# Turning a batch's last 64 logits with small products, between two heads' values

## The chip, the cores and the metric

One core of a Trainium2 chip runs the whole program. The metric is the device time of one execution in microseconds; below it is the median of three runs. A profile of one execution shows what every engine did.

## The reference

Decaying causal attention over 8 batches of 8 heads (576 tokens, head width 64), whose output (4608 x 512) goes through a soft mixture of 8 experts with 4 slots each:

```
scores = scale * (q @ k^T) + cum[i] - cum[j], masked above the diagonal
attn   = softmax(scores);  x = attn @ v             (all heads side by side: 512 columns)
logits = x @ phi                                     (4608 x 32)
d = softmax of logits over all tokens   ->  slot_input = d^T @ x
slot_out = relu(slot_input @ w1) @ w2                (per expert)
c = softmax of logits over the 32 slots ->  out = c @ slot_out
```

So every batch's logits are needed twice: against the running maximum over tokens (to dispatch tokens to slots), and token by token over the 32 slots (to combine slots).

## The kernel before, in words

The order of every engine's work is written out by hand: an engine issues its instructions in the order in which the program's lines name it, and waits on semaphores for the others.

**The main loop** (lines 725 to 865) goes over g = 1 to 31, two heads ("pair") at a time, four pairs to a batch. In a pair, TensorE computes the first scores of heads to come (`s1`, line 230, into three score banks `s` that rotate), the second scores of the pair's own heads (`s2`, lines 283 and 284, into a ring of three banks), turns the output of the pair before (`px`, line 342) and ends with the value products (`s3`, line 315), head 0's and then head 1's. ScalarE takes the exponentials (`expo`, line 290), rounds keys and queries of a later pair (`round_k`, `round_q`, lines 183 and 188) and copies; VectorE takes row maxima (`tops`) and normalizes heads (`norm`, lines 330 to 335); GpSimd masks (`causal`) and subtracts low parts (`low_k`, `low_q`).

**The logits of a batch b** lie as 32 slots on each of four lane groups; 576 tokens are 4 x 128 and a last 64, which stands in columns 128 to 192 of lanes 0 to 31. The steps are spread over the next batch's pairs, numbered w = 0 to 3: at the end of w = 0 the product with phi (`logits`, line 389); in w = 1 the copy to `LG` (`weigh`), the maximum (`mgroup`, `mtop`) and its broadcast to all lanes by four products 32 wide and 2 columns long (`mcast`, lines 420 to 424), the weights `EX = exp(LG - max)` (`weigh2`, line 431), the running sum `lrun` (`total`, line 446), and `tokens`; in w = 2 `dispatch` (line 475), which uses the turned weights `LD`.

**`tokens`** turns both tables from slots on lanes to tokens on lanes, in a score bank called `tk`: three 128-column turns by the identity (lines 456, 457, 459), the second of EX's columns 128 to 256 alone. That one turn serves both tables, since the last 64 weights and the last 64 raw logits had been copied to other lanes of `EX` columns 192 to 256 before (GpSimd copies, lines 397 and 432). The turned rows of the first table go to `LD` (line 464, ScalarE), those of the second are read from the bank by `combine(b, 0)` on VectorE (lines 495, 496), which stands early in w = 2 and frees the bank. `combine` steps 1 and 2 follow with the next batch.

**The last batch** does the same in the tail (lines 870 to 905), where LD is copied on VectorE, where `split` and `cols` turn the combinations of all batches into weights of the output products (lines 696, 711), and where `tokens(b, 0)` stands between the expert products (line 938).

A float32 product is issued as two passes, each with its own weight load; a turn is issued once.

Of the kernel before, what the change touches and what calls it, by code (L numbers as in the profile page):

```python
# [9 lines left out]
AF = mybir.ActivationFunctionType  # L10
# [65 lines left out]
def attn_softmoe(ctx: ExitStack, tc: tile.TileContext, qk, v, f, phi, w1, w2, cst, out):  # L76
    nc = tc.nc
# [102 lines left out]
    def round_k(g, *hs):  # L180
        if pair(g):
            for h in hs or range(2):
                nc.scalar.copy(WA[g % 3][0:64, S * h : S * h + S], RAW[g % 3][64:128, h])  # L183

    def round_q(g, *hs):
        if pair(g):
            for h in hs or range(2):
                nc.scalar.copy(YA[g % 3][0:64, h, 64:640], RAW[g % 3][0:64, h])  # L188
# [202 lines left out]
    def weigh(b):  # L391
        if batch(b):
            plg = st["lg", b]
            if b < B - 1:
                nc.scalar.copy(LG[:, 0:128], plg[:, 0:128])
                nc.scalar.copy(LG[0:32, 128:192], plg[0:32, 128:192])
                nc.gpsimd.tensor_copy(EX[96:128, 192:256], LG[0:32, 128:192])  # L397
            else:
                nc.scalar.copy(LG[:, 0:192], plg[:, 0:192])
                nc.gpsimd.tensor_copy(EX[96:128, 192:256], LG[0:32, 128:192])  # L400

    def mgroup(b):
        if not batch(b):
# [22 lines left out]
    def weigh2(b):  # L426
        if not batch(b):
            return
        mb = st["mb", b]
        if b < B - 1:  # L430
            nc.scalar.activation(EX[:, 0:192], LG[:, 0:192], AF.Exp, bias=mb[:, 1:2], accum_out=mb[:, 2:3])
            nc.gpsimd.tensor_copy(EX[0:32, 192:256], EX[0:32, 128:192])
        else:
            nc.scalar.activation(EX[:, 0:192], st["lg", b][:, 0:192], AF.Exp, bias=mb[:, 1:2])
            nc.vector.tensor_copy(EX[0:32, 192:256], EX[0:32, 128:192])
        if b > 0:
            nc.scalar.activation(mb[:, 3:4], st["mb", b - 1][:, 1:2], AF.Exp, bias=mb[:, 1:2], scale=-1.0)

    def total(b):
        if not batch(b):  # L440
            return
        mb = st["mb", b]
        if b == 0:
            nc.scalar.copy(lrun, mb[:, 2:3])
        elif b < B - 1:
            nc.scalar.activation(lrun, lrun, AF.Identity, scale=mb[:, 3:4], bias=mb[:, 2:3])
        else:
            nc.vector.scalar_tensor_tensor(lrun, in0=lrun, scalar=mb[:, 3:4], in1=mb[:, 2:3], op0=ALU.mult, op1=ALU.add)

    def tokens(b, *ns):  # L450

        if not batch(b):
            return
        pm = turn() if b == B - 1 else scratch(False, f"tk{b}")
        if 1 in ns:
            nc.tensor.transpose(pm[:, 0:128], EX[:, 0:128], ident)
        nc.tensor.transpose(pm[:, 128:256], EX[:, 128:256], ident)
        if 0 in ns:
            nc.tensor.transpose(pm[:, 256:384], LG[:, 0:128], ident)
        if 0 in ns:  # L460
            st["tok", b] = pm
        if 1 in ns:
            copy = nc.scalar.copy if b < B - 1 else nc.vector.tensor_copy
            copy(LD, pm[:, 0:160].rearrange("p (t s) -> p t s", t=NBLK))
# [74 lines left out]
    nc.gpsimd.memset(WA[0][96:98].bitcast(F32), -1.0)  # L539
    nc.gpsimd.memset(YA[0][0:64, :, 0:64].bitcast(F32), 0.0)  # L540
    nc.gpsimd.memset(LG[:, 128:256], -1.0e30)
    nc.gpsimd.memset(EX[:, 192:256], 0.0)
    nc.vector.tensor_scalar(fx, fx, 1e-4, 1.0, op0=ALU.max, op1=ALU.min)
    nc.scalar.activation(fx, fx, AF.Ln)
    for h in range(2):
# [137 lines left out]
    def split(b, *parts):  # L683

        if 0 in parts:
            if b < 2:
                CW[b] = tp.tile([P, NBLK, 2, 2, NS], F32R, name=f"cw{b}")
            else:
                spare = quarter[NRES - 9 + b][:, 0 : 4 * NBLK * NS].bitcast(F32R)
                CW[b] = spare.rearrange("p (t o r s) -> p t o r s", t=NBLK, o=2, r=2)  # L690
        hi, lo = (CW[b][:, :, :, r] for r in range(2))
        two = ctok[:, b].rearrange("p t (o s) -> p t o s", o=1).broadcast_to([P, NBLK, 2, NS])
        if 0 in parts:
            nc.scalar.copy(hi, two)
        if 1 in parts:
            nc.vector.tensor_tensor(lo, two, hi.bitcast(F32), op=ALU.subtract)
# [28 lines left out]
    for g in range(1, NG):  # L725
        h0, h1 = 2 * g, 2 * g + 1
        u0, u1 = h0 + 3, h0 + 4
        b, w = divmod(g - 4, NPAIR)
        c = b - 1 if w == 0 else b if (b, w) == (B - 2, 3) else None
        if g < 4:  # L730
            load_v(g + 1)
            load_qk(g + 3)
        else:
            load_qk(g + 3)
            load_v(g + 1)
        if w == 1:
            weigh(b)
        low_q(h0 + 2)
        low_q(h1 + 2)
        s2(h0, 0)  # L740
        expo(h0, 0)
        norm(h0 - 1)
        if w == 1:
            mgroup(b)
        if w == 2:
            combine(b, 0)
        s1(u0, 2)
        tops(u0, 2)
        s2(h0, 1)
        expo(h0, 1)  # L750
        s1(u0, 3)
        tops(u0, 3)
        s2(h0, 2)
        expo(h0, 2)
        if g > 1:
            px(g - 1, 0)
            px(g - 1, 3)
        else:
            round_k(3, 0)
            round_q(3, 0)  # L760
        s1(u0, 0, 1)
        tops(u0, 0, 1)
        if g > 1:
            px(g - 1, 1)
        s2(h0, 3)
        if g > 1:
            xcopy(g - 1, (0, 3))
            px(g - 1, 2)
            xcopy(g - 1, (1, 2))
        s2(h0, 4)  # L770
        s1(u0, 4, 5)
        s2(h0, 5)
        expo(h0, 3)
        tops(u0, 4, 5)
        causal(h0)
        low_k(h0 + 2)
        if w == 1:
            mtop(b)
        s2(h1, 0)
        expo(h1, 0)  # L780
        if g == 1:
            for t in (0, 3, 1, 2):
                px(0, t)
        px(g - 1, 4)
        if g == 1:
            xcopy(0, (0, 3))
            xcopy(0, (1, 2))
        if g == 1:
            xcopy(0, (4,))
        s1(u1, 2)  # L790
        tops(u1, 2)
        s2(h1, 1)
        expo(h1, 1)
        s1(u1, 3)
        tops(u1, 3)
        s2(h1, 2)
        mturn(g + 1)
        mrows(g + 1)
        expo(h1, 2)
        if g > 1:  # L800
            xcopy(g - 1, (4,))
        s1(u1, 0, 1)
        tops(u1, 0, 1)
        s2(h1, 3, 4)
        s1(u1, 4, 5)
        s2(h1, 5)
        expo(h1, 3)
        tops(u1, 4, 5)
        causal(h1)
        low_k(h1 + 2)  # L810
        if g == 1:
            round_k(3, 1)
            round_q(3, 1)
        load_cum(g + 3)
        dup_q(g + 2)
        dup_k(g + 2)
        if 2 <= g < NRES + 2:
            wload(g - 2)
        if g == 29:
            sides[2].close()  # L820
            p2 = fresh(ctx, "p2", 2)
            wstream(*p2, RAW[30 % 3])
        if g == 30:
            sides[1].close()
            xp = ctx.enter_context(tc.tile_pool(name="xp", bufs=1))
            X.append(xp.tile([P, NBLK, 256], F32, name="X3"))
            p0 = fresh(ctx, "p0", 1)
            p1 = fresh(late, "p1", 3)
            wstream(*p0, *p1, RAW[31 % 3])
        if g == 31:  # L830
            sides[0].close()
            with tc.using_default_side("right"):
                tp = ctx.enter_context(tc.tile_pool(name="tp", bufs=1))
            cT = tp.tile([P, sum(CUT)], F32R, name="cT")
            wstream(tp.tile([P, QW], F32, name="w36"))
        if w == 1:
            mcast(b)
        if c is not None:
            combine(c, 1)
        if w == 2 and b < B - 2:  # L840
            dispatch(b, *range(NBLK))
        if g == NG - 1:
            st["lg", B - 1] = scratch(False, f"lg{B - 1}")
            nc.vector.memset(st["lg", B - 1][:, 128:192], -1.0e30)
        round_k(g + 3)
        if w == 1:
            weigh2(b)
            total(b)
        round_q(g + 3)
        if c is not None:  # L850
            combine(c, 2)
        s3(g, VALUES[:30])
        norm(h0)
        if g == 31:
            logits(B - 1, 0, 1)
            wstream(XTS[:, 0:QW], PTS[:, 0:QW])
            split(0, 0)
            split(1, 0)
        s3(g, VALUES[30:])
        if w == 0:  # L860
            logits(b, *range(NPAIR))
        if w == 1:
            tokens(b, 0, 1)
        if g == 28:
            wstream(RAW[29 % 3])
    logits(B - 1, 2)
# [26 lines left out]
    next(c[0])  # L893
    next(c[0])
    next(c[0])
    tokens(b, 1)
    split(1, 1)
    next(c[1])
    next(c[1])
    nc.vector.tensor_reduce(mb[:, 2:3], EX[:, 0:192], axis=AX.X, op=ALU.add)  # L900
# [237 lines left out]
```

## Time and profile before

| | us |
|---|---|
| median of 3 runs (388.98 to 390.79) | 390.42 |
| time of the profiled execution | 389.33 |
| its span, first to last instruction | 387.6 |
| TensorE busy (matmul row) | 368.5 (95%) |
| VectorE, ScalarE, GpSimd busy | 279.2, 274.3, 254.8 |

The matmul row counts a matmul from its start to a modelled end, longer than the step to the next start, so a row near 100% can still hold short holes; they are found by the starts. The main loop takes some 9 to 10 us a pair and ends near 315 us; the last batch's dispatch is at 326 us, the expert products run from 328 to 361, the output after.

### The profile page before, as it was taken

To read this page: it belongs to the slowest core of one execution; us is meant where nothing else is said; L and a number is where in the kernel's file an instruction comes from. 1 tells how busy PE (TensorE), PEld (TensorE's weight loads), DVE (VectorE), ACT (ScalarE), POOL (GpSimd) and SP (SyncE) were. 2 spreads that over 40 slices of the span, in tenths; PEclk is the share of its full clock that TensorE was granted. 3 is DMA by queue.
4 is the path that set the end of the run, shared out by engine and by line. 5 is a ranking of instruction groups with operands and counts; after the bars stand their busy time and mean duration, and the time that the engine had idled before them with its cause. 6 is when DMAs were issued, how large, how long until landed. Compare 5 with 4: busy or idle time off the path is not lost.

```text
span 387.6 us, 15148 instructions
## 1 busy us (share of the span) xinstructions
PE 368.5 (95%) x5863; PEld 330.8 (85%) x5863; DVE 279.2 (72%) x1079; ACT 274.3 (71%) x670; POOL 254.8 (66%) x357
## 2 busy tenths in 40 slices
PE   8999999999999999999999999999999998999870
PEld 8889999999999999999999999999999985567640
DVE  7878787878887888788878887888787535441671
ACT  8969887878787878787878787878787553021560
POOL 4987887878787878787878787878787821000000
PEclk9999999999999999999999999999999999999995
DMA  6785878777777777777777777777777989996798
GB/s 206 199 203 153 241 223 269 201 226 201 231 210 218 214 214 215 215 216 213 214 215 217 212 215 215 215 216 214 212 224 208 280 316 361 416 418 258 269 391 317
DMA packets 34344, 93.72 MB, mean 242 GB/s; under 512 B 4266, under 2 KB 8288, under 8 KB 34272
## 3 DMA queue, kind: packets, MB, share of 16 engines
q1 hardware_dynamic: 34272, 92.75, 76.8%
q8 instruction: 46, 0.75, 0.8%
q14 instruction: 26, 0.21, 0.2%
HBM read 63.93 MB, written 9.73 MB: 190 GB/s over the span
## 4 chain that ended last, share of the span: by engine, by line
PE 89%; DMA 3%; ACT 2%; DVE 2%; issue 1%; POOL 1%; SPq 0%; ACTq 0%; POOLq 0%; DVEq 0%
PE pv L315 23%; PE ring L283 14%; PE s L230 13%; PE ring L284 12%; PE pv L342 4%; PE pv L978 4%; PE more L938 4%; PE lg L389 3%; PE ring L511 2%; PE ds L475 2%; DMA out<-RAW 2%; PE ring L1055 1%; DMA YA<-mr 1%; ACT PTS L290 1%; DMA WA<-cumd 1%
## 5 line engine op out<-in xcount | busy, mean ns | idle before, releaser
L290 ACT ACTIVATE PTS<-ring 128x320 f32<-128x320 f32 (+2 forms) x256 | 119.1, 501 | 39.1 <-PE ring L284 31.8
L283 PE MATMUL ring<-YA,WA 67*128 67x320 f32 (+9 forms) x384 | 119.0, 323 | 0.1
L246 DVE CUSTOM_DVE_ANT_0 s<-s,mask 128x320 f32<-128x320 f32 (+3 forms) x256 | 109.6, 446 | 5.6 <-PE s L230 0.9
L284 PE MATMUL ring<-YB,WB 128*128 128x320 f32 (+4 forms) x384 | 110.4, 296 | 0.0
L315 PE MATMUL pv<-V,PTS 128*64 128x65 f32 x3200 | 102.3, 223 | 0.1
L315 PEld LDWEIGHTS pv<-V,PTS 128*64 128x64 f32 x3200 | 97.2, 138 | 3.1 <-issue 1.6
L230 PE MATMUL s<-WA,YA 66*128 66x288 f32 (+9 forms) x384 | 97.9, 310 | 1.0 <-ACT YA L188 0.4
L209 POOL TENSOR_TENSOR WB<-RAW,WB 64x576 fp32r<-64x576 f32 x64 | 90.4, 1413 | 10.9 <-ACT WA L570 4.6
L214 POOL TENSOR_TENSOR YB<-RAW,YA 64x576 fp32r<-64x576 f32 x64 | 89.7, 1419 | 2.6 <-POOL EX L397 0.2
L283 PEld LDWEIGHTS ring<-YA,WA 67*128 67x128 f32 (+3 forms) x384 | 69.0, 181 | 5.8 <-issue 2.1
L284 PEld LDWEIGHTS ring<-YB,WB 128*128 128x128 f32 (+1 forms) x384 | 70.0, 182 | 0.0
L230 PEld LDWEIGHTS s<-WA,YA 66*128 66x128 f32 (+1 forms) x384 | 62.9, 190 | 6.8 <-ACT PTS L290 1.7
L301 POOL TENSOR_SCALAR_AFFINE_SELECT PTS<-PTS 128x128 f32<-128x128 f32 (+1 forms) x128 | 31.5, 268 | 21.9 <-ACT PTS L290 20.3
L246 DVE DVE_READ_ACCUMULATOR2_ANT MT<- 128x1 fp32r x310 | 44.0, 142 | 0.0
L183 ACT CAST WA<-RAW 64x576 fp32r<-64x576 f32 x64 | 40.2, 669 | 3.0 <-DMA RAW<-in_qk 2.1
L298 POOL TENSOR_SCALAR_AFFINE_SELECT PTS<-PTS 128x384 f32<-128x384 f32 x64 | 33.4, 523 | 12.2 <-ACT PTS L290 8.3
L188 ACT CAST YA<-RAW 64x576 fp32r<-64x576 f32 x64 | 40.3, 670 | 0.4
L246 DVE CUSTOM_DVE_ANT_0 s<-s,mask,MT 128x288 f32<-128x288 f32 x62 | 32.6, 526 | 10.0 <-PE s L230 1.4
L342 PE MATMUL pv<-cs,X 128*128 128x128 f32 x155 | 36.5, 272 | 0.0
L330 DVE TENSOR_SCALAR rl<-pv 128x5 f32<-128x5 f32 x64 | 10.5, 164 | 35.0 <-PE pv L315 24.7
L335 DVE TENSOR_TENSOR X<-pv,rl 128x320 f32<-128x320 f32 (+1 forms) x65 | 31.5, 486 | 2.4 <-DMA YA<-mr 0.3
L244 DVE TENSOR_REDUCE MT<-s 128x1 fp32r<-128x288 f32 x62 | 27.9, 450 | 0.0
(220 smaller groups left out, 386.5 us busy)
## 6 DMA issues: line engine op xcount, KB each, us to landing
w<-in_w SPq DMA_DIRECT2D x45, 512.0 KB
RAW<-in_qk SPq DMA_DIRECT2D x31, 576.0 KB
V<-in_v SPq DMA_DIRECT2D x32, 325.0 KB
YB<-YA SPq DMA_DIRECT2D x30, 288.0 KB
WB<-WA SPq DMA_DIRECT2D x30, 288.0 KB
p<-in_w SPq DMA_DIRECT2D x6, 512.0 KB
out<-RAW SPq DMA_DIRECT2D x6, 512.0 KB
out<-p SPq DMA_DIRECT2D x5, 512.0 KB
```

The source lines that it names most:

```text
L183: nc.scalar.copy(WA[g % 3][0:64, S * h : S * h + S], RAW[g % 3][64:128, h])
L188: nc.scalar.copy(YA[g % 3][0:64, h, 64:640], RAW[g % 3][0:64, h])
L209: nc.gpsimd.tensor_tensor(t[0:64], RAW[g % 3][64:128, h], t[64:128].bitcast(F32), op=ALU.subtract)
L214: nc.gpsimd.tensor_tensor(YB[g % 2][64:128, h], RAW[g % 3][0:64, h], YA[g % 3][0:64, h, 64:640].bitcast(F32), op=ALU.subtract)
L230: nc.tensor.matmul(t[:, o : o + w], ya[0:m, h, 128 * blk : 128 * blk + 128], wa[0:m, j0 : j0 + w], start=True, stop=True)
L246: nc.vector.tensor_tensor_reduce(out=t[:, o : o + w], in0=t[:, o : o + w], in1=mask[:, m0 : m0 + w], scale=1.0, scalar=top.bitcast(F32) if ...
L283: nc.tensor.matmul(o, wa[0:m, j0 : j0 + n], ya[0:m, h, 64 + i0 : 64 + i0 + w], start=True, stop=False)
L284: nc.tensor.matmul(o, wb[:, j0 : j0 + n], yb[:, h, i0 : i0 + w], start=False, stop=True)
L290: nc.scalar.activation(PT[i % 2][:, SEG_O[bank] : SEG_O[bank] + at], t[:, 0:at], AF.Exp, scale=0.125)
L298: nc.gpsimd.affine_select(d3, d3, pattern=[[0, 3], [1, 128]], compare_op=ALU.is_ge, fill=0.0, base=0, channel_multiplier=-1)
L315: nc.tensor.matmul(pvv[h][64 * u : 64 * u + 64, t, :], PT[h][:, at : at + 64], V[:, g % 2, c, 65 * h : 65 * h + 65], start=(c == 0), stop= ...
L342: nc.tensor.transpose(pm[:, 0:128], x[:, t, 128 * (p % 2) : 128 * (p % 2) + 128], ident)
```

## The change

The last 64 columns of each table are turned by a product of their own instead of a shared third turn: `x[0:32, 128:192]` (32 lanes deep, 64 wide) times a 32 x 32 identity, once onto lanes 0 to 63 and once onto lanes 64 to 127 of the bank. The copies to spare lanes of `EX` and the memset of these go. `tokens` handles table 0 (raw logits) first, then table 1 (weights). In w = 1 `tokens` and `combine(b, 0)` move between the value products of head 0 and head 1; one of the two key casts and both query casts move behind them; `combine(b, 0)` leaves w = 2. The running sum moves from ScalarE to GpSimd. In the tail `split(1, 1)` moves ahead of `tokens(b, 1)`.

```diff
@@ weigh, weigh2
-                nc.gpsimd.tensor_copy(EX[96:128, 192:256], LG[0:32, 128:192])      (both branches)
-            nc.gpsimd.tensor_copy(EX[0:32, 192:256], EX[0:32, 128:192])
-            nc.vector.tensor_copy(EX[0:32, 192:256], EX[0:32, 128:192])             (last batch)
@@ total
-            nc.scalar.activation(lrun, lrun, AF.Identity, scale=mb[:, 3:4], bias=mb[:, 2:3])
+            nc.gpsimd.tensor_scalar(lrun, lrun, mb[:, 3:4], mb[:, 2:3], op0=ALU.mult, op1=ALU.add)
@@ tokens
-        if 1 in ns:
-            nc.tensor.transpose(pm[:, 0:128], EX[:, 0:128], ident)
-        nc.tensor.transpose(pm[:, 128:256], EX[:, 128:256], ident)
-        if 0 in ns:
-            nc.tensor.transpose(pm[:, 256:384], LG[:, 0:128], ident)
+        for n in sorted(ns):
+            x, o = (LG, 256) if n == 0 else (EX, 0)
+            nc.tensor.transpose(pm[:, o : o + 128], x[:, 0:128], ident)
+            for u in range(2):
+                nc.tensor.matmul(pm[64 * u : 64 * u + 64, 224 - 96 * n : 256 - 96 * n], x[0:32, 128:192], ident[0:32, 0:32], start=True, stop=True)
@@ setup
-    nc.gpsimd.memset(EX[:, 192:256], 0.0)
@@ main loop
-        if w == 2:
-            combine(b, 0)
...
-        round_k(g + 3)
         if w == 1:
+            round_k(g + 3, 0)
             weigh2(b)
             total(b)
-        round_q(g + 3)
+        else:
+            round_k(g + 3)
+            round_q(g + 3)
         if c is not None:
             combine(c, 2)
         s3(g, VALUES[:30])
         norm(h0)
...
+        if w == 1:
+            tokens(b, 0, 1)
+            combine(b, 0)
+            round_k(g + 3, 1)
+            round_q(g + 3)
         s3(g, VALUES[30:])
         if w == 0:
             logits(b, *range(NPAIR))
-        if w == 1:
-            tokens(b, 0, 1)
@@ tail
+    split(1, 1)
     tokens(b, 1)
-    split(1, 1)
```

## Rows read from the trace of the kernel before

**Rows 1.** The page's 40 slices of the span: granted TensorE clock in tenths.
```profile
PEclk9999999999999999999999999999999999999995
```

**Rows 2.** The page's chain of waits that ended last, share of the span by engine.
```profile
PE 89%; DMA 3%; ACT 2%; DVE 2%; issue 1%; POOL 1%; SPq 0%; ACTq 0%; POOLq 0%; DVEq 0%
```

**Rows 3.** Timeline (start us, length us, instructions merged) of TensorE, end of second pair, batch 3.
```profile
147.98 0.52 PE L315 MATMUL pv<-V,PTS 128*64 128x65 f32 x12
148.43 0.33 PE L456 MATMUL tk<-cs,EX 128*128 128x128 f32 x1
...
149.08 0.37 PE L284 MATMUL ring<-YB,WB 128*128 128x448 f32 x1
```

**Rows 4.** Timeline of TensorE, end of the third pair, without turns.
```profile
158.89 0.23 PE L315 MATMUL pv<-V,PTS 128*64 128x65 f32 x2
...
159.36 0.37 PE L284 MATMUL ring<-YB,WB 128*128 128x448 f32 x1
```

**Rows 5.** Timeline of TensorE in the tail: one-lane products, turns and the broadcast's products.
```profile
320.61 0.21 PE L877 MATMUL more<-row,fin 1*1 1x32 f32 x2
320.75 0.52 PE L475 MATMUL more<-X,LD 128*32 128x128 f32 x9
...
322.79 0.44 PE L711 MATMUL ring<-cs,cw 128*128 128x128 f32 x2
323.16 0.24 PE L421 MATMUL ring<-cs,row 1*32 1x2 f32 x8
323.33 0.55 PE L711 MATMUL ring<-cs,cw 128*128 128x128 f32 x3
```

**Rows 6.** Timeline of TensorE: the first value products of batch 3's second pair.
```profile
145.36 0.34 PE L315 MATMUL pv<-V,PTS 128*64 128x65 f32 x4
```

**Rows 7.** Timeline of TensorE, third pair's third score bank: batch 0, then batch 3.
```profile
73.75 0.38 PE L342 MATMUL pv<-cs,X 128*128 128x128 f32 x2
73.89 0.39 PE L230 MATMUL s<-WA,YA 66*128 66x320 f32 x1
...
150.15 0.38 PE L342 MATMUL pv<-cs,X 128*128 128x128 f32 x2
150.61 0.39 PE L230 MATMUL s<-WA,YA 97*128 97x320 f32 x1
```

**Rows 8.** Waits of the weight loads, whole span: us in total, times, longest.
```profile
PEld s L230 <- ACT PTS L290: 1.7, 6, 0.3
```

**Rows 9.** Timelines of ScalarE, VectorE and GpSimd, batch 3's second pair and after.
```profile
146.00 1.24 ACT L183 CAST WA<-RAW 64x576 fp32r<-64x576 f32 x2
147.27 0.46 ACT L431 ACTIVATE EX<-LG,mb 128x192 f32<-128x192 f32 x1
147.63 0.19 ACT L431 ACTIVATION_READ_ACCUMULATOR EX<-LG,mb 128x1 f32 x1
...
148.04 0.39 ACT L446 ACTIVATE lrun<-lrun,mb 128x1 f32<-128x1 f32 x1
...
146.42 0.15 DVE L422 COPY mb<-ring 128x1 f32<-128x1 f32 x1
...
149.78 0.33 DVE L495 TENSOR_REDUCE sm<-tk 128x5 f32<-128x160 f32 x1 [0.25 <-ACT LD L464]
150.15 0.32 DVE L496 TENSOR_TENSOR ctok<-tk,sm 128x160 f32<-128x160 f32 x1
...
148.31 0.23 POOL L432 COPY EX<-EX 32x64 f32<-32x64 f32 x1
```

**Rows 10.** Timelines of TensorE and VectorE in the tail, the last batch's weights.
```profile
324.13 0.33 PE L456 MATMUL more<-cs,EX 128*128 128x128 f32 x1 [0.26 <-ACT EX L434]
...
325.49 0.44 PE L711 MATMUL more<-cs,cw 128*128 128x128 f32 x2 [0.82 <-DVE cw L696]
325.86 0.54 PE L475 MATMUL pv<-X,LD 128*32 128x128 f32 x12
...
324.72 0.32 DVE L464 COPY LD<-more 128x160 f32<-128x160 f32 x1 [0.42 <-PE more L457]
```

More of the change, by code (lines that the diff above doesn't have):

```diff
@@ L396, in weigh @@
                 nc.scalar.copy(LG[0:32, 128:192], plg[0:32, 128:192])
-                nc.gpsimd.tensor_copy(EX[96:128, 192:256], LG[0:32, 128:192])
             else:
                 nc.scalar.copy(LG[:, 0:192], plg[:, 0:192])
-                nc.gpsimd.tensor_copy(EX[96:128, 192:256], LG[0:32, 128:192])
     def mgroup(b):
@@ L431, in weigh2 @@
             nc.scalar.activation(EX[:, 0:192], LG[:, 0:192], AF.Exp, bias=mb[:, 1:2], accum_out=mb[:, 2:3])
-            nc.gpsimd.tensor_copy(EX[0:32, 192:256], EX[0:32, 128:192])
         else:
             nc.scalar.activation(EX[:, 0:192], st["lg", b][:, 0:192], AF.Exp, bias=mb[:, 1:2])
-            nc.vector.tensor_copy(EX[0:32, 192:256], EX[0:32, 128:192])
         if b > 0:
```

## The prediction

> **What bounds the kernel now.** First the granted clock and the chain of waits: the clock of TensorE stands in the top tenth in all slices but the last [rows 1], and 89% of the chain that ended last is TensorE [rows 2]. So time is read from TensorE's own timeline, pair of heads by pair of heads: what matters is the step from the start of one matmul to the start of the next. The reader is to see two kinds of step. Two value products on the two lane halves start together, and the next two 0.058 us later (twelve in 0.52 us, one lasting 0.22-0.23) [rows 3]. But where the shape of the products changes, a hole opens: from the last value product (148.50 less 0.22, so 148.28) to the first turned tile 0.15 us [rows 3], from two 128-column turns to the 32-column broadcast products and back [rows 5]. These holes are TensorE idle inside, though the modelled busy row hides them. All 7 batches b = 0 to 6 do this work in the second pair after the batch, the eighth in the tail.
>
> **The change, part by part.** Durations are from the profiled execution (span 387.6 us, its time 389.33 us, 1.1 us under the median 390.42 of the three runs); differences are added to both.
>
> *Turning, in the stream of TensorE (b = 0 to 6).* Before, three 128-column turns stand behind all value products: 148.28 to the second product of the next pair at 149.08 is 0.80 us [rows 3], and a pair with no turns needs 158.89 to 159.36, 0.47 us [rows 4]. So they cost 0.33 us, what they wait for the removed GpSimd copy included. Now the work stands between two heads' values, and the stream goes: value products, LG's turn, two small products, EX's turn, two small products, value products. Each small product is 32 lanes deep, 64 wide, 32 columns; float32 products are issued as two passes (the broadcast's four are x8), turns as one [rows 5]. The steps:
> - value products to LG's turn: 0.15 [rows 3].
> - a turn with a change of shape on both sides: two of them take 322.79 to 323.16, 0.37, of which the second adds 0.11 (three in 0.55 less two in 0.44) [rows 5]: 0.26.
> - a block of two small products up to the next shape. The trace of before has none. From below, the broadcast's block, 2 columns on 32-wide tiles: 323.16 to 323.33, 0.17. From above: the step between the first two pairs of 64-wide value products behind a change is 0.11 (four in 0.34, two in 0.23) [rows 4, 6], and after the last pass of a 32-column product on one lane the next shape starts 0.12 later (0.14 from 320.61 to 320.75 less some 0.03 between its two passes) [rows 5]: 0.23. I take 0.20, between ends that are close.
> - EX's turn and its block: 0.26 + 0.20.
> - the first pair of value products after a change takes 0.11 instead of 0.06 [rows 3, 6]: 0.05; and the ordinary step of 0.06 would have been there without the change.
>
> Sum 0.15 + 0.26 + 0.20 + 0.26 + 0.20 + 0.05 - 0.06 = 1.06 us, less the 0.33 saved at the pair's end: +0.73 us, seven times: **+5.1 us** (0.17 to 0.23 a block: 4.7 to 5.5). Nothing hides it: value products wait behind it on the same engine, and no other engine's delay stands next to it.
>
> The Trainium skill, TensorEngine Tiling (Array Packing), section Tiling Modes, says that changing the tiling mode, not merely the tile, drains the engine; it names no price. The trace agrees: 0.37 us from the first of two turns to the broadcast against 0.11 for a further turn [rows 5], while lane halves of one mode alternate 0.058 us apart [rows 3]. By the rule alone this stretch goes from one drain to six, which speaks against the change; the prices above are the rows' own.
>
> *Does EX come in time?* The wait of TensorE on EX moves from behind all values to the middle, so every later value product is queued behind it. The maximum is in SBUF at 146.57 (146.42 + 0.15); ScalarE has now one of its two key casts ahead of EX instead of both (two in 1.24 from 146.00, so free at 146.62), and EX with its accumulator takes 147.27 to 147.82 (147.63 + 0.19), 0.55 [rows 9]: ready at 147.2. TensorE has 30 products (60 passes) from 145.36 [rows 6], so to 145.36 + 0.11 + 28 x 0.058 = 147.1, and reaches EX's turn 0.15 + 0.26 + 0.20 later at 147.7. Cover 0.5 us; cost 0.
>
> *ScalarE and VectorE.* ScalarE loses the running sum (0.39 us [rows 9]) and waits instead in the middle for the turns before it copies LD; the other three casts then stand behind that copy: LD at about 148.2 to 148.5, three casts of 0.62 to 150.3, where the next pair's first exponential, 0.73 us later than today, wants it at about 150.2. No DMA is issued by a moved step, and the casts moved later are copied on by DMA only at the end of the next pair. The 0.1 is hidden by the ring of three banks, as the later start of before was. VectorE's two steps on the turned logits end today at 150.47 (150.15 + 0.32) [rows 9], and there TensorE stands: the bank with the turned logits is the one that the next pair's third score bank takes. From the two turns at 150.15 to the score product at 150.61 is 0.46 us, while in the batch-0 pair, where no running sum is in ScalarE's queue, the same step is 73.75 to 73.89, 0.14 [rows 7]. With the combination done inside the second pair the bank is free early: -0.32 us for b = 1 to 5 (the wait's row counts six with 1.7 us together, one of them elsewhere [rows 8]; batch 6's next pair shows no hole): **-1.6 us**. Next late after that is nothing: the steps behind are at TensorE's own pace.
>
> *GpSimd.* Two copies a batch of 0.23 us go [rows 9], a one-column multiply-add comes, in the place of the second copy. Not in this trace; from the nearest rows 0.23 (that copy), at the far end ScalarE's 0.39 for the same sum [rows 9]; only the next batch waits for the sum, and the queue loses 0.46 of copies. Both ends cost 0. No gain either, TensorE's waits for these copies being in the 0.33. The start's memset of EX goes: 0.
>
> *Tail, batch 7.* Today EX is copied to the spare lanes, turned (324.13 is when EX's exponential lets TensorE start), LD is copied on VectorE at 324.72 for 0.32, the split of a combination follows, its turns wait for it until 325.49, and the dispatch starts at 325.86 [rows 10]. With the split moved ahead of LD's copy, it runs while VectorE waits anyway. Then EX's turn 324.13 + 0.26, second pass of the small products + 0.11 and its 0.2 us: 324.70; LD's copy 324.74 to 325.06; the split's turns are through before that; dispatch at 325.11: **-0.75 us**, all on the chain up to the expert products. The logits' turn there becomes a turn and a block, 0.46 for 0.37 (two turns, [rows 5]): **+0.1 us**.
>
> Sum: 5.1 - 1.6 - 0.75 + 0.1 = **+2.8 us**: 392.1 against 389.33, or 393.2 us against the median of 390.42.
>
> **Rivals.**
> *A, no slower: the small products don't change the engine's mode for a price.* If each product joined at the pace of products of one mode, a block is two steps of 0.06 and a turn 0.11, so 2 x (0.11 + 0.12) = 0.46; +0.13 a batch, 0.9 in all; with -1.6, -0.75 and -0.14 for the tail's second block the time is 388.8, a little faster or the same. For it: value products alternate between lane halves free of charge [rows 3]. Against it: broadcast products, just as shallow, show the hole on both sides, and so do the products on a single lane [rows 5]. It decides where the insertion takes 0.65 us instead of 1.06: seven times 0.32 are the 2.25 us given back.
> *B, worse: the relief does not come.* If the bank is freed late again (LD's copy now waits for TensorE in the middle of ScalarE's queue, and VectorE's steps wait for LD's copy, as their releaser is today [rows 9]), the 0.32 x 5 stay: 394.8. It decides if the second of these steps ends after the next pair's two turns. By the times above LD's copy ends at 148.5 and VectorE's steps at 149.2, before the next pair even starts (149.9): against it.
>
> **How the numbers follow.** Forecast 0.56, its own range 392.2 to 394.2; A 0.28; B 0.16. About 0.5% (1.95 us) is what a measurement of this kernel can tell from no change, so the lines are 388.5 and 392.4. Slower: 0.42 of the forecast's and 0.13 of B's, 0.55. The same: 0.14 of the forecast's, 0.16 of A's, 0.03 of B's, 0.33. Faster: 0.12, all A's. Range 389.0 to 395.6: it leaves out the lower half of A and the upper end of B.
>
> **What would show it.** Right: in the second pair of each batch, 1.0 to 1.1 us from the 30th value product's pass to the 31st's, with holes of 0.1 us before and after each block; 0.47 us at that pair's end; no hole before the third score bank in the next pair; the dispatch of the last batch 0.7 us sooner after EX. Wrong: blocks that run into the turns without holes (A), a TensorE wait for EX in the middle, or a wait for VectorE at the score bank (B).

## The result, and the profile after

The changed kernel takes 392.12 us (median of six, 391.85 to 392.34) against 389.44 us for the kernel before, run beside it (median of six, 388.59 to 390.79): a ratio of 1.0064, interval 1.0042 to 1.0086, slower by 2.7 us. Run again later beside the best versions below, it took 392.25 against 388.9: 1.0081 (1.0064 to 1.0099), 3.35 us. The forecast was 393.2, its sum +2.8 us; it stands on 390.42, the median of three runs of the kernel before, where six give 389.44.

The page's clock row is the same digit by digit as [rows 1], and the chain of waits [rows 2] has still more of TensorE in it. The kernel is bound as it was.

```profile
span 390.1 us, 15241 instructions
...
PE 91%; DMA 3%; DVE 2%; issue 1%; ACT 1%; ACTq 0%; DVEq 0%
```

TensorE's timeline of the changed kernel (start, length, instructions merged), first batch 3's second pair and the pair behind it, then the tail; it answers to [rows 3, 4, 7, 10]:

```profile
147.38 0.46 PE L315 MATMUL pv<-V,PTS 128*64 128x65 f32 x10
147.77 0.33 PE L453 MATMUL tk<-cs,LG 128*128 128x128 f32 x1
148.03 0.30 PE L455 MATMUL tk<-cs,LG 32*64 32x32 f32 x4
148.26 0.33 PE L453 MATMUL tk<-cs,EX 128*128 128x128 f32 x1
148.52 0.30 PE L455 MATMUL tk<-cs,EX 32*64 32x32 f32 x4
148.75 0.34 PE L315 MATMUL pv<-V,PTS 128*64 128x65 f32 x4
...
149.91 0.23 PE L315 MATMUL pv<-V,PTS 128*64 128x65 f32 x2
...
150.38 0.37 PE L284 MATMUL ring<-YB,WB 128*128 128x448 f32 x1
...
151.46 0.38 PE L342 MATMUL pv<-cs,X 128*128 128x128 f32 x2
151.60 0.39 PE L230 MATMUL s<-WA,YA 97*128 97x320 f32 x1
...
327.30 0.33 PE L453 MATMUL more<-cs,EX 128*128 128x128 f32 x1 [0.26 <-ACT EX L431]
327.56 0.30 PE L455 MATMUL more<-cs,EX 32*64 32x32 f32 x4
327.79 0.44 PE L706 MATMUL more<-cs,cw 128*128 128x128 f32 x2
328.29 0.54 PE L471 MATMUL pv<-X,LD 128*32 128x128 f32 x12
...
334.38 0.33 PE L453 MATMUL ring<-cs,LG 128*128 128x128 f32 x1
...
334.88 0.64 PE L936 MATMUL more<-w,EX 128*32 128x256 f32 x8
```

Read it by starts. The last value product before the turns starts at 147.38 + 0.46 - 0.22 = 147.62. From there the steps are 0.15 to LG's turn, 0.26 to its small products, 0.23 to EX's turn, 0.26, and 0.23 to the next value product, 1.13 us in all. The step from the pair's last two value products to the second product of the next pair is 149.91 to 150.38, 0.47, as in a pair without turns. The hole before the third score bank is gone: 151.46 to 151.60, 0.14 where [rows 7] has 0.46, and no wait row of that place [rows 8] is left. In the tail the dispatch comes 0.99 us after EX's turn starts (328.29 less 327.30), where [rows 10] has 1.73. The logits' turn and block there take 0.50 (334.38 to 334.88); two turns, the bound taken for before, take 0.37 [rows 5].

ScalarE, GpSimd and VectorE of the same stretch, and VectorE in the tail:

```profile
147.21 0.46 ACT L429 ACTIVATE EX<-LG,mb 128x192 f32<-128x192 f32 x1
147.57 0.19 ACT L429 ACTIVATION_READ_ACCUMULATOR EX<-LG,mb 128x1 f32 x1
...
148.87 0.29 ACT L460 COPY LD<-tk 128x160 f32<-128x160 f32 x1 [0.93 <-PE tk L455]
...
148.65 0.34 POOL L442 TENSOR_SCALAR lrun<-lrun,mb 128x1 f32<-128x1 f32 x1
...
149.56 0.32 DVE L492 TENSOR_TENSOR ctok<-tk,sm 128x160 f32<-128x160 f32 x1
...
327.91 0.33 DVE L460 COPY LD<-more 128x160 f32<-128x160 f32 x1 [0.72 <-PE more L455]
```

EX is complete at 147.57 + 0.19 = 147.76, and its turn starts at 148.26: 0.50 us of cover. VectorE's second step on the turned logits ends at 149.88, long before 151.46. ScalarE idles 0.93 us ahead of LD's copy, and TensorE's rows behind it show no wait for that.

### The profile page after: what moved, and what is told of

Read it like the earlier page. It is cut to its first block, busy times and chain, and to the rows that moved or that the text cites. A ratio compares the mean times of both kernels' runs of the same rounds, so it can differ in the third digit from the quotient of the medians.

```text
span 390.1 us, 15241 instructions
## 1 busy us (share of the span) xinstructions
PE 372.0 (95%) x5918; PEld 332.7 (85%) x5918; DVE 280.0 (72%) x1078; ACT 273.7 (70%) x664; POOL 253.8 (65%) x347
## 4 chain that ended last, share of the span: by engine, by line
PE 91%; DMA 3%; DVE 2%; issue 1%; ACT 1%; ACTq 0%; DVEq 0%
PE pv L315 26%; PE ring L283 15%; PE s L230 13%; PE ring L284 13%; PE pv L342 4%; PE pv L976 4%; PE more L936 4%; PE lg L389 3%; DMA out<-RAW 3%; PE ds L471 2%; PE tk L453 1%; PE tk L455 1%; DMA PTS<-in_f 1%; PE ring L507 1%; PE ring L1053 1%
## 5 line engine op out<-in xcount | busy, mean ns | idle before, releaser
L315 PE MATMUL pv<-V,PTS 128*64 128x65 f32 x3200 | 103.6, 223 | 0.0
```

The costliest lines, as they stand in the source:

```text
L315: nc.tensor.matmul(pvv[h][64 * u : 64 * u + 64, t, :], PT[h][:, at : at + 64], V[:, g % 2, c, 65 * h : 65 * h + 65], start=(c == 0), stop= ...
```

## The experiments

Nine other kernels, and the changed one again. Ratios are to the kernel before, run on the same chip with them; 9 and 10 ran on another chip than 1 to 8. Differences in us are of medians. One number compares the insertions: from the start of LG's turn to the first value product behind the block, 147.77 to 148.75 in the changed kernel, 0.98 us (0.15 us before that step is common). A second one gives the main loop: from the first value product of batch 0's second pair to that of batch 6's third pair, seven insertions apart, it is 307.28 - 68.96 = 238.32 us before and 310.46 - 68.26 = 242.20 after, +3.9.

**1. Is it the changes of shape?** Both turns first, then all four small products; the work is the same, with two changes of shape fewer:

```diff
         for n in sorted(ns):
             ...
             nc.tensor.transpose(pm[:, o : o + 128], x[:, 0:128], ident)
+        for n in sorted(ns):
             for u in range(2):
                 nc.tensor.matmul(...)
```

> The changed kernel with the same instructions in another order inside the turning: both tables' turns, then all four small products (two changes of shape fewer per batch). Theory (a change of shape costs TensorE some 0.1 us): from the last value product before the insertion to the first behind it 0.15 + 0.37 (two turns) + some 0.40 (eight passes and the way out) = 0.92 us instead of 1.14 us in the changed kernel's trace, so -0.22 x 7 = -1.6 us against the changed kernel: ratio to the kernel before about 1.002. Rival (the time is that of the passes and weight loads themselves, wherever they stand): the insertion stays at 1.14 us and the ratio at 1.0064.

390.61 us, 1.0041 (1.0028 to 1.0053), 1.6 us under the changed kernel run again in 8, as expected. TensorE in batch 3:

```profile
147.41 0.33 PE L453 MATMUL tk<-cs,LG 128*128 128x128 f32 x1
147.58 0.27 PE L453 MATMUL tk<-cs,EX 128*128 128x128 f32 x1
147.78 0.30 PE L457 MATMUL tk<-cs,LG 32*64 32x32 f32 x4
147.92 0.28 PE L457 MATMUL tk<-cs,EX 32*64 32x32 f32 x4
148.13 0.34 PE L315 MATMUL pv<-V,PTS 128*64 128x65 f32 x4
```

The next value product starts at 148.13, so the stretch is 0.72, 0.26 less than 0.98 with the same instructions. A turn behind a turn costs 0.17, a block in front of a block 0.14. So the price lies in the changes, and rival A's free alternation is not there.

**2. Does a product of the values' tile join them?** The small products 128 lanes deep, still 64 wide and 32 columns, and first. Depth and place change together:

```diff
-                nc.tensor.matmul(..., x[0:32, 128:192], ident[0:32, 0:32], ...)
+                nc.tensor.matmul(..., x[:, 128:192], ident[:, 0:32], ...)
```

> The changed kernel with the small products taken 128 lanes deep instead of 32 (64 columns of weights by 128 x 32 of the identity, whose lower lanes are zero), the four products first, then the two turns. Theory: a 128-deep, 64-wide product has the shape of the value products, so the four join them at some 0.06 us a step of two passes, and only the way into the turns and the way back are left: 4 x 0.06 + 0.15 + 0.37 + 0.05 - 0.06 = 0.75 us from the last value product to the next in place of 1.14, so -0.39 x 7 = -2.7 us against the changed kernel: ratio to the kernel before about 0.9995. Rival (the passes and weight loads cost what they cost): four times the depth and the same number of passes, so 1.14 us or more, ratio 1.0064 or more.

390.25 us, 1.0029 (1.0015 to 1.0042), 2.0 us under the changed kernel where 2.7 were expected. TensorE in batch 3, then in batch 5, with ScalarE's cast there:

```profile
147.09 0.40 PE L315 MATMUL pv<-V,PTS 128*64 128x65 f32 x8
147.33 0.26 PE L454 MATMUL tk<-cs,LG 128*64 128x32 f32 x4
147.47 0.31 PE L454 MATMUL tk<-cs,EX 128*64 128x32 f32 x4
147.71 0.33 PE L457 MATMUL tk<-cs,LG 128*128 128x128 f32 x1
...
262.93 0.26 PE L454 MATMUL tk<-cs,LG 128*64 128x32 f32 x4
263.60 0.31 PE L454 MATMUL tk<-cs,EX 128*64 128x32 f32 x4 [0.41 <-ACT EX L429]
...
262.30 0.67 ACT L183 CAST WA<-RAW 64x576 fp32r<-64x576 f32 x1 [0.55 <-DMA RAW<-in_qk]
```

The last two value products start at 147.09 + 0.40 - 0.22 = 147.27, the first deep product at 147.33: 0.06, the pace of the value products among themselves. So 32 columns instead of 65 open no hole. The depth does: in 1 the step from a block of 32 lanes to the value products, just as wide, is 0.21 (147.92 to 148.13) where a block in front of another of its kind takes 0.14. The width of the tile does too: the second deep block takes 0.24 up to the turn (147.47 to 147.71; 0.22 in 6), though both are 128 lanes deep, and that is no less than the 0.23 of a block of 32 lanes. In the changed kernel every change but the last is one of width, between a turn and a 64-wide product; deep products between the turns were not tried. In batch 5 the key cast came 0.55 us late behind its load, and the second block waited 0.67 us after the first instead of 0.14: moving EX's products ahead of the turns had used up the cover. That is some 0.5 of the 0.7 us that were missing. The Trainium skill, TensorEngine Tiling (Array Packing), section Tiling Modes, says that a change of mode, not of tile, drains the engine. The traces agree (0.06 without, 0.15 to 0.26 for a step with one), and the price is what they add.

**3. Three turns in the middle, copies restored, the late one on VectorE.** This asks whether the place or the small products cost:

```diff
+            nc.vector.tensor_copy(EX[0:32, 192:256], EX[0:32, 128:192])
...
+        if b < B - 1:
+            nc.tensor.transpose(pm[:, 256:384], LG[:, 0:128], ident)
+            nc.tensor.transpose(pm[:, 0:128], EX[:, 0:128], ident)
+            nc.tensor.transpose(pm[:, 128:256], EX[:, 128:256], ident)
```

> The changed kernel with the small products of batches 0 to 6 replaced by the shared third turn of the kernel before, with copies to the spare lanes (the second on VectorE), all at the new place between two heads' values; the tail is the changed kernel's. Theory: the place costs only a way in and a way out: 0.15 + 0.17 + 0.11 + 0.20 + 0.05 - 0.06 = 0.62 us instead of 1.14, so -0.52 x 7 = -3.6 us against the changed kernel: ratio to the kernel before about 0.997. Rival (it is the place between the heads that costs, through waits for EX): the insertion stays near 1.1 us, ratio 1.006.

394.89 us, 1.0143 (1.0118 to 1.0168): a miss in sign. GpSimd, VectorE and TensorE in batch 3:

```profile
148.54 1.40 POOL L209 TENSOR_TENSOR WB<-RAW,WB 64x576 fp32r<-64x576 f32 x1
...
148.98 1.01 DVE L431 COPY EX<-EX 32x64 f32<-32x64 f32 x1 [0.65 <-ACT EX L430]
...
149.13 0.27 PE L455 MATMUL tk<-cs,EX 128*128 128x128 f32 x1
150.05 0.33 PE L456 MATMUL tk<-cs,EX 128*128 128x128 f32 x1 [0.65 <-DVE EX L431]
```

The turns join as expected, but the third waits for the copy, which takes 1.01 us and ends at 149.99, 0.05 after GpSimd's subtraction (149.94). All seven copies take 0.97 to 1.08. The question was not answered, so it was put again in 7.

**4. The running sum alone.** The kernel before with one line of the change:

```diff
-            nc.scalar.activation(lrun, lrun, AF.Identity, scale=mb[:, 3:4], bias=mb[:, 2:3])
+            nc.gpsimd.tensor_scalar(lrun, lrun, mb[:, 3:4], mb[:, 2:3], op0=ALU.mult, op1=ALU.add)
```

> The kernel before with one edit of the change: the running sum on GpSimd instead of ScalarE. Theory (the hole at the third score bank in the third pair of a batch is ScalarE's late copy of LD, late by the running sum's 0.39 us): the hole of 0.32 us goes in batches 1 to 5, -1.6 us: ratio 0.996. Rival (the hole goes only when the combination's first step is moved out of the third pair): ratio 1.000, the hole stays.

386.95 us, 0.9946 (0.9927 to 0.9966), -1.8 us. The score bank of [rows 7], batch 3:

```profile
149.10 0.38 PE L342 MATMUL pv<-cs,X 128*128 128x128 f32 x2
149.24 0.48 PE L230 MATMUL s<-WA,YA 97*128 97x320 f32 x2
```

The step is 0.14, and the main loop is 236.58 us long, -1.74: the whole relief comes from ScalarE's queue being shorter by one sum. It does not need the insertion.

**5. The two gains without the insertion.** 4, with the tail's split moved ahead and LG turned first:

```diff
+        if 0 in ns:
+            nc.tensor.transpose(pm[:, 256:384], LG[:, 0:128], ident)
         if 1 in ns:
             ...
-        if 0 in ns:
-            nc.tensor.transpose(pm[:, 256:384], LG[:, 0:128], ident)
...
+    split(1, 1)
     tokens(b, 1)
-    split(1, 1)
```

> The kernel before, its three turns left at the pair's end, with what the change brought beside them: the running sum on GpSimd, the tail's split ahead of the last weights' turn, and the raw logits' turn first so that the copy to spare lanes hides behind it. Theory: -2.1 us (as the sum alone measured), -0.7 us in the tail, -0.06 x 7 = -0.4 us from the order of turns: about -3.2 us, ratio 0.992. Rival (the tail's gain needs the copy of the last weights to go as well, and the copy is long done by the time of its turn): ratio 0.9946, as the sum alone.

385.99 us, 0.9919 (0.9902 to 0.9935): it beats both kernels, and by 6.3 us the changed one (392.25 on the same chip). Its tail:

```profile
321.66 0.33 PE L458 MATMUL more<-cs,EX 128*128 128x128 f32 x1 [0.26 <-ACT EX L434]
...
322.64 1.30 PE L475 MATMUL pv<-X,LD 128*32 128x128 f32 x40
```

The dispatch comes 0.98 us after EX, as in the changed kernel, with the copy of EX to the spare lanes still there. What gives 0.75 in the tail is the split's place, not the missing copy. The order of the turns gave nothing: the pair's end is 0.76 us instead of 0.80, but the main loop is 236.56 us, as in 4, where 0.4 less was expected.

**6. Deep products at the pair's end.** 4, the split moved, the copies and the memset of EX removed, and the products of 2 behind all values:

```diff
+                nc.tensor.matmul(..., x[:, 128:192], ident[:, 0:32], start=True, stop=True)
...
-        nc.tensor.transpose(pm[:, 128:256], EX[:, 128:256], ident)
```

> The kernel before with the sum on GpSimd and the tail's split moved, and no copies to spare lanes: behind all value products come four 128-deep small products and then two turns. Theory (a product in the value products' shape joins them at some 0.06 us a step, and the change of shape at a pair's end is there anyway): four steps of 0.06 for one turn of 0.11 and a wait of 0.06, +0.07 us a batch, so -2.1 - 0.7 + 0.5 = -2.3 us, ratio 0.994. Rival (small products cost by themselves, whatever their shape): 0.4 us a batch more than the turn they replace, ratio 1.000.

386.92 us, 0.9943 (0.9925 to 0.9961). TensorE in batch 3:

```profile
147.99 0.69 PE L315 MATMUL pv<-V,PTS 128*64 128x65 f32 x18
148.51 0.26 PE L454 MATMUL tk<-cs,LG 128*64 128x32 f32 x4
148.60 0.29 PE L454 MATMUL tk<-cs,EX 128*64 128x32 f32 x4
...
149.30 0.37 PE L284 MATMUL ring<-YB,WB 128*128 128x448 f32 x1
```

From the last two value products (148.46) to the second product of the next pair it is 0.84 us, against 0.80 in [rows 3] and 0.76 in 5, which differs from this kernel by these products, the copies and the memset alone. Even joined, two blocks are no cheaper than the one turn that they replace.

**7. Three turns in the middle, the late copy on ScalarE.** As 3, with

```diff
-            nc.vector.tensor_copy(EX[0:32, 192:256], EX[0:32, 128:192])
+            nc.scalar.copy(EX[0:32, 192:256], EX[0:32, 128:192])
```

> As the kernel with three turns at the new place, with the second copy to spare lanes on ScalarE instead of VectorE, where it took 1.01 us beside GpSimd's subtraction and held TensorE's last turn up. Theory (the place costs a way in and a way out, and that kernel was slow by this copy alone): the insertion takes 0.62 to 0.70 us instead of the changed kernel's 1.14, so some -3.3 us against the changed kernel. Rival (the place costs, through waits for EX or for ScalarE): no gain against the changed kernel.

389.22 us, 1.0003 (0.9991 to 1.0015), -3.0 us against the changed kernel. TensorE in batch 3:

```profile
147.71 0.33 PE L454 MATMUL tk<-cs,LG 128*128 128x128 f32 x1
147.88 0.27 PE L455 MATMUL tk<-cs,EX 128*128 128x128 f32 x1
148.03 0.33 PE L456 MATMUL tk<-cs,EX 128*128 128x128 f32 x1
148.29 0.33 PE L315 MATMUL pv<-V,PTS 128*64 128x65 f32 x3
```

The next value product starts at 148.29: 0.58 us instead of 0.98. So of the loss 0.40 a batch is the small products. The rest is in the main the place: with the 0.15 ahead of it and the displaced step, as in the table below, three turns cost 0.72 between two heads' values and 0.33 at the pair's end [rows 3, 4], where the value products give way to 128-wide scores in any case. Of this, 0.1 is a wait for the copy: the third turn's weights are loaded 0.05 us after the copy ends (147.97), 0.12 after the second's, while in batch 6 they follow the second's at once and the stretch is 0.48 (301.36 to 301.84).

**8. The changed kernel again**, on the chip of 5, 6 and 7:

> The changed kernel itself, on the same chip as the other kernels of this round, so that differences to it are taken from one place. From the first comparison 1.0064 [1.0042, 1.0086]; by the two traces' main loop and tail without the first 45 us (where the two profiled executions differ by 0.7 us before any batch is turned) +3.2 us, ratio 1.008.

392.25 us, 1.0081 (1.0064 to 1.0099).

**9. The tail's split back behind EX's turn**, in the changed kernel:

```diff
-    split(1, 1)
     tokens(b, 1)
+    split(1, 1)
```

> The changed kernel with the tail's split of a combination back behind the last weights' turn, as in the kernel before. Theory (the tail's gain is the split's place): LD's copy, then the split of 0.48 us, then its two turns, and the dispatch some 0.8 us later than in the changed kernel: ratio to the kernel before 1.0102 instead of 1.0081. Rival (the gain is the copy to spare lanes that went): no more than 0.2 us later, ratio 1.0085.

393.55 us, 1.0122 (1.01 to 1.0145). Its tail:

```profile
327.28 0.33 PE L453 MATMUL more<-cs,EX 128*128 128x128 f32 x1 [0.25 <-ACT EX L431]
...
328.67 0.44 PE L706 MATMUL more<-cs,cw 128*128 128x128 f32 x2 [0.83 <-DVE cw L691]
329.04 0.32 PE L471 MATMUL pv<-X,LD 128*32 128x128 f32 x4
```

The dispatch starts 1.76 us after EX's turn, 0.77 later than in the changed kernel: the term of the tail, by itself. The time rose by 1.3 us over that of 8 and the span of the profiled execution by 0.9 (391.0 against 390.1); what the rest is stays open.

**10. One more turn and block.** EX's turn and its two products repeated behind the block in batches 0 to 6:

```diff
+        if b < B - 1:
+            nc.tensor.transpose(pm[:, 0:128], EX[:, 0:128], ident)
+            for u in range(2):
+                nc.tensor.matmul(pm[64 * u : 64 * u + 64, 128:160], EX[0:32, 128:192], ident[0:32, 0:32], start=True, stop=True)
```

> The changed kernel with one turn and one block of two small products more in each of batches 0 to 6: the weights are turned a second time onto the same place. Theory (a turn and a block cost 0.26 + 0.23 us of TensorE each time, and nothing hides them): +0.49 x 7 = +3.5 us on the changed kernel's 392.25, ratio to the kernel before 1.017. Rival (part of the insertion is hidden by work that TensorE would have waited for anyway): less than +2 us, ratio under 1.013.

396.31 us, 1.0189 (1.0171 to 1.0208). TensorE in batch 3:

```profile
149.26 0.33 PE L453 MATMUL tk<-cs,LG 128*128 128x128 f32 x1
...
150.25 0.33 PE L457 MATMUL tk<-cs,EX 128*128 128x128 f32 x1
150.51 0.30 PE L459 MATMUL tk<-cs,EX 32*64 32x32 f32 x4
150.74 0.34 PE L315 MATMUL pv<-V,PTS 128*64 128x65 f32 x4
```

From LG's turn to the values it is 1.48 us, 0.50 more than 0.98, and seven times 0.50 is 3.5 us. The main loop is longer by just that (245.66 us against 242.20). The time rose by 4.1 over the 392.25 of 8 (in its own profile the first 45 us and the last pair, too, were some 0.7 slower). The price goes into the time in full; what the 0.6 above it is stays open.

## Why the prediction was right

| Term | Predicted | Measured in the traces |
|---|---|---|
| insertion, one batch | 1.06 | 1.12 (1.13 + 0.05 - 0.06) |
| saved at the pair's end | 0.33 | 0.33 |
| both, seven batches | +5.1 | +5.5 (7 x 0.79) |
| third score bank, five batches | -1.6 | -1.6 (5 x 0.32) |
| dispatch in the tail | -0.75 | -0.74 |
| the tail's logits | +0.1 | +0.13 |
| sum | +2.8 | +3.3 |

- *Changes of shape as the price: right.* The holes stand where they were expected; 1 shortens them by changing the order alone, 10 adds them once more at the same price. The turn was 0.26 as taken. The block was 0.23, the upper of the two bounds; the 0.20 taken between them was 0.03 low, 0.4 us over two blocks and seven batches.
- *EX in time: right*, 0.50 us of cover as worked out, and 2 shows that it is not much: there one late load ate it.
- *The bank relief: right in size.* The prediction put it down to the combination's earlier place; 4 shows that the sum's move is enough without it. The steps that free the bank ended some 0.2 us later than forecast (149.88 in a pair whose value products began at 145.87 and not at 145.36, so 149.37 where 149.2 was forecast), but 1.6 us before the bank was wanted. So rival B did not come.
- *GpSimd's sum: right.* It took 0.34 us, inside 0.23 to 0.39, in a queue with room.
- *The split in the tail: right*, shown by 9 with the block and by 5 without it.
- *Rival A: false.* An insertion of 0.65 us, the prediction's mark for it, is where gains and losses would have been even; it took 1.12. A's own sum was too good for it: its 0.46 leaves out the way into the first turn and out of the block (0.15 + 0.05 - 0.06), 1 us over seven batches, so that A stood for some 389.8 and not 388.8.

The terms sum to +3.3, the second comparison measured 3.35 and the first 2.7. That the first came within 0.1 us of the forecast's 2.8 is partly luck: the blocks were taken 0.4 us too cheap. The spans of the two profiled executions differ by 2.5 us only. Of that gap, 0.7 us lies in the first 45 us, before any batch is turned: the kernel before was slower there in its profiled execution. The fourth block of value products starts at 49.92 in it, at 49.22 in the changed kernel, and at 49.23 in 4, which differs from the kernel before by the sum alone. Its other runs spread over 2.2 us, and the intervals of the two comparisons overlap from 1.0064 to 1.0086. Why some of its executions start slower was not tried.

What the sum hid is the more useful part. The change is three edits with separate effects: the sum on GpSimd (-1.8 us by 4), the split's place (-0.77 by 9) and the insertion, which pays about 6 us (the 6.3 between 5 and 8, which differ by it and by the logits' block) to save two GpSimd copies that cost TensorE next to nothing: at the pair's end the turns take 0.33 us in the kernel before and 0.29 in 5 (0.76 less 0.47), which keeps both.

## What to carry to other kernels

On an engine that is busy throughout, count the changes of shape (a tile's depth or width) in its stream before the instructions: here a turn costs 0.11 to 0.17 us behind another turn and 0.26 between two changes, and a block of two products on 32 lanes 0.23 between two changes, more than the full turn behind another that it replaces. Take a mixed change apart and run each edit alone: two of three here were gains, and the version with these two is 0.9919 of the time before. A copy on an engine with room was free here, and removing such a copy is worth only what the new path costs less.

## What the runs showed that was not expected

In 3 a VectorE copy of 32 x 64 within on-chip memory took 1.01 us, while the same form takes 0.18 in the tail of the kernel before, where GpSimd runs nothing:

```profile
324.11 0.18 DVE L435 COPY EX<-EX 32x64 f32<-32x64 f32 x1 [0.49 <-ACT EX L434]
```

In batch 3 it started 0.44 us after a GpSimd subtraction (148.98 against 148.54) and ended 0.05 after it; in all seven batches it ended 0.04 to 0.06 after one (in batch 0 at 71.66 against 71.60). The same copy on ScalarE in 7 took 0.24 to 0.25 in all seven batches. So the copy waited for GpSimd's operation. The Trainium skill, SBUF — State Buffer, section SBUF: two separate sides, says that VectorE in its two-port mode and GpSimd hold one pair of ports exclusively for a whole instruction, whichever starts first. Starts and ends agree; that these ports are the cause was not tried by itself.
